# Attention into a two-layer block: order of the block sums, of the words' square, of the late parts' rests and of a load

## The chip, the cores and the metric

The kernel runs on one core of one Trainium2 chip. The core has a matrix engine (TensorE, PE in the profile; PEld is its weight load), VectorE (DVE), ScalarE (ACT), GpSimd (POOL), and SyncE (SP), which here only issues DMAs. Each engine works through its own instructions in order and waits on semaphores for the others. The metric is the device time of one execution in microseconds: the median of several.

## The reference

Eight sequences of 448 positions and 12 heads of 64 go through attention; the result, 3584 x 768, goes through two large products with a squared ReLU between them.

```python
q_n, k_n = rmsnorm(q, g_q), rmsnorm(k, g_k)        # x / sqrt(mean(x*x) + 1e-6) * g
scores = (q_n @ k_n.T) / sqrt(64)
attn = exp(scores - max(scores));  attn = attn / (sum(attn) + 1e-9)
x = (attn @ v) laid out as 3584 x 768
h = x @ w_in                                       # 768 x 2048, w_in arrives as float64
g = s * maximum(h, 0) ** 2 + b
out = g @ w_out                                    # 2048 x 768, w_out arrives as float64
```

## The kernel before, in words

**Three stages.** Stage A (0 to about 600 us of the profiled span) is attention, two heads (a *pair*) at a time, 48 pairs, in *slots*: four slots to a pair, 192 slots and some at either end. Stage B (about 605 to 1127 us) is x @ w_in, stage C (to the end) g @ w_out.

**Stage A.** A table, `STAGES` (L30), and the calls of `at` (L379 to L392) say in which slot each step of a pair is issued; within a slot, steps stand in the order in which they were put down. Steps that matter here, for pair p, with s0 = 4p: `load_kq` (L210, DMA of k, q and v of the pair, 704 KB, into one of six buffers `kqv`; the buffer is free when `weigh`, L286, of pair p-6 has read it); `scale` (L223: ScalarE multiplies k by a constant, L226, then GpSimd multiplies k and q by the rows' norms, L230); `score` and `maximum` (L237, L249: products into the one PSUM tile `sh`, then VectorE takes maxima, L253); `score_t` and `exponent`; `weigh`; `take` (L308: ScalarE copies the weighted sums to `uz` and the sums of exponentials to `sz`, L316, one buffer); `gather` (L319, DMA `s_d` from `sz`) two slots later, `fetch` (L322, DMA `zt` from `s_d`) two slots after that, `invert` (L326, VectorE, L328 and L329) three slots after that, then `put_z`, `get_z`, `divide` (GpSimd, L344) and `put_x`. Most DMAs are issued by SP, in order; `raw` (L189) by ScalarE's queue. Every DMA carries one of eight semaphores (DMAHW0 to DMAHW7) in turn, and is issued only when the DMA that carried the same one before it has landed.

**Float64 weights.** `words_of` (L107) makes float32 out of the two 32-bit words of a float64: three VectorE operations shift and join them (L110, L112, L114), ScalarE squares the high word (L116), and a fourth VectorE operation (L119) zeroes what is too small, by that square. Of w_in this happens in stage A (`convert`, L349; its square is one row apart from the other steps, a slot each). Of w_out, 32 pieces are done in stage B (`convert_out`, L567): a piece's load is started in one block and all its operations follow in the next. Each two pieces share a tile `o` (one buffer, pool "c"); after the second, GpSimd makes three sums (L138 to L140) and a DMA stores them to `w_d`.

**Stage B.** 56 *blocks*, n = 0 to 55, four to a *run* (14 runs). `ffn_in` (L468) gives TensorE 63 products for a block, into four PSUM banks of two parts each; there are eight banks, so block n+1 can begin when the sums of block n-1 have read theirs. `rectify` (L508) of block n-1 is issued after the products of block n: `add_up` (L482) makes four block sums out of seven parts (parts 0 and 1 lie in the first bank, 2 and 3 in the second): three ScalarE copies (L487 to L489), VectorE sums (L485), a fourth ScalarE copy with a changed sign (L495), more VectorE sums, eight in all; then ScalarE's ReLU (L524) and a DMA to `r_d`. Where two engines read one PSUM bank, the second waits until the first has done with it. Behind `rectify` in each engine's order stand the words of w_out (in the first three blocks of a run), and `steps` (L705): in the second block of a run GpSimd's sums for two of the next run's three inputs and the first `s_split` (L454: ScalarE rounds, L150, VectorE takes the rest, L152), in the third block GpSimd's sums of the third input, in the last block two more `s_split`. In blocks 25 to 28 `steps` also makes four late parts of w_in ready: 12 `tin_split` (L541), ScalarE rounding and VectorE taking the rest. Each part goes into the buffer of a part that TensorE has just read for the last time, and is read three blocks after the block in which it is made. The pieces of w_out are begun from block 4 on, but not in a run's third block; the last is finished in block 46.

**Stage C.** 112 rounds of 21 products, `multiply` (L632); after each eighth, `combine` (L651) makes the block sums by the same `add_up`, here with one PSUM bank a part, and stores them.

The order on every engine is the order of the calls in the program (`manual_schedule`, L676): nothing is moved by a scheduler.

## Time and profile before

| | |
|---|---|
| time, median of 3 runs | 1562.89 us (1559.93 to 1564.72) |
| profiled execution, its own time | 1566.36 us |
| its span | 1564.6 us |
| PE / PEld busy | 1385.4 us (89%) / 1101.2 us (70%) |
| DVE / ACT / POOL busy | 1000.1 / 773.4 / 807.5 us |
| DMA | 253.71 MB, mean 162 GB/s |
| granted PE clock, mean | 0.952 |

The span is the time between the first and the last instruction of the profiled execution; 1.8 us lie around it. A group's line gives busy time and mean time of one instruction, then, behind the bar, how long the engine stood idle just before such instructions and what ended that. In a timeline row the idle time before the first instruction of the row stands in brackets. The granted clock is 1.00 at 2.4 GHz and 0.50 at 1.2 GHz.

### The profile page before, as it was taken

What the parts mean: (1) busy time and instruction counts of PE and PEld (TensorE: products, weight loads), DVE (VectorE), ACT (ScalarE), POOL (GpSimd) and SP (SyncE); (2) the same over time, 40 slices, a digit from 0 to 9 for tenths busy, and PEclk for the clock granted to TensorE, in tenths of its full rate; (3) what the DMA queues carried; (4) which work ended last, traced back from release to release, by engine and by line L of the source; (5) the groups of instructions that cost most, each with busy time, mean ns of one, the idle gap of its engine ahead of it and who ended that gap; (6) DMA issues with size and microseconds to landing.
All of it is one profiled execution on the core that took longest, in us unless ns stands there. A gap on an engine that the chain in (4) does not pass through costs nothing.

```text
span 1564.6 us, 26152 instructions
## 1 busy us (share of the span) xinstructions
PE 1385.4 (89%) x9760; PEld 1101.2 (70%) x9760; DVE 1000.1 (64%) x1546; ACT 773.4 (49%) x1132; POOL 807.5 (52%) x719
## 2 busy tenths in 40 slices
PE   2699898899898998989887789889889999999999
PEld 1344444444343446888887789879879999999999
DVE  3467575666555633566666867676687767767776
ACT  2367666666564653344444533444554444444443
POOL 5457677777666634443433433433035654654653
PEclk6799999999999999999999998999989999999999
DMA  6468786878787833444547444554653332332331
GB/s 204 127 180 227 199 237 193 232 204 246 216 230 209 231 103 105 152 166 147 169 145 263 151 160 143 166 172 140 215 187 95 116 100 82 117 99 83 115 99 63
DMA packets 172367, 253.71 MB, mean 162 GB/s; under 512 B 54544, under 2 KB 122832, under 8 KB 172240
## 3 DMA queue, kind: packets, MB, share of 16 engines
q1 hardware_dynamic: 165904, 231.86, 48.8%
q10 hardware_dynamic: 6336, 20.19, 4.4%
q8 instruction: 76, 1.25, 0.3%
q14 instruction: 51, 0.42, 0.1%
HBM read 183.06 MB, written 68.76 MB: 161 GB/s over the span
## 4 chain that ended last, share of the span: by engine, by line
PE 47%; DMA 16%; DVE 12%; issue 11%; ACT 6%; POOL 5%; SPq 2%; ACTq 0%; POOLq 0%; DVEq 0%
PE m L642 24%; PE st L273 6%; PE av L294 6%; PE h L476 4%; DMA zt<-s_d 3%; DVE r L485 3%; DMA raw<-in_dram 3%; PE sh L244 3%; PE av L301 2%; ACT s L150 2%; DVE nmx L253 2%; DVE s L152 2%; PE st L277 2%; DMA s<-x_d 2%; DMA i_d<-ri 2%
## 5 line engine op out<-in xcount | busy, mean ns | idle before, releaser
L476 PE MATMUL h<-s,tin 128*128 128x256 f32 x3528 | 457.9, 293 | 68.6 <-DVE r L485 39.2
L476 PEld LDWEIGHTS h<-s,tin 128*128 128x128 f32 x3528 | 446.3, 198 | 80.8 <-DVE r L485 46.3
L642 PE MATMUL m<-tout,gh 128*128 128x384 f32 x1568 | 405.6, 340 | 8.2 <-ACT gh L626 7.9
L642 PEld LDWEIGHTS m<-tout,gh 128*128 128x128 f32 x1568 | 288.0, 190 | 9.7 <-ACT gh L626 8.7
L253 DVE TENSOR_REDUCE nmx<-sh 112x2 fp32r<-112x896 f32 x192 | 207.8, 1084 | 109.9 <-PE sh L244 106.9
L642 PE MATMUL m<-tout,gl 128*128 128x384 f32 x784 | 266.7, 340 | 5.7 <-DVE gl L627 5.7
L284 ACT ACTIVATE e<-st 128x896 f32<-128x896 f32 x192 | 176.3, 919 | 146.9 <-PE st L277 146.6
L606 POOL TENSOR_TENSOR g<-g 128x256 f32<-128x256 f32 x112 | 94.4, 843 | 230.7 <-DVE g L605 230.7
L626 ACT CAST gh<-g 128x896 fp32r<-128x896 f32 x112 | 105.4, 942 | 175.1 <-POOL g L610 101.3
L273 PE MATMUL st<-kqv 64*128 64x448 f32 x768 | 188.2, 563 | 0.0
L627 DVE TENSOR_TENSOR gl<-g,gh 128x896 fp32r<-128x896 f32 x112 | 140.8, 1258 | 58.6 <-ACT gh L626 58.6
L244 PEld LDWEIGHTS sh<-kr 64*112 64x112 f32 x384 | 55.8, 278 | 168.2 <-issue 58.1
L294 PE MATMUL av<-e,kqv 128*32 128x448 f32 x1536 | 165.1, 547 | 7.5 <-ACT uz L317 5.2
L485 DVE TENSOR_TENSOR r<-r,h 128x256 f32<-128x256 f32 x408 | 144.0, 415 | 37.0 <-ACT r L495 26.3
L244 PE MATMUL sh<-kr 64*112 64x448 f32 x384 | 94.2, 481 | 80.1 <-DVE nmx L253 41.7
L152 DVE TENSOR_TENSOR s<-s,s 128x1792 fp32r<-128x1792 f32 x42 | 84.5, 2037 | 122.6 <-ACT s L150 114.1
L642 PEld LDWEIGHTS m<-tout,gl 128*128 128x128 f32 x784 | 149.0, 190 | 7.8 <-DVE gl L627 7.8
L277 PE MATMUL st<-shq,row 64*128 64x448 f32 x384 | 145.7, 742 | 3.8 <-DMA shq<-nmx 3.8
L344 POOL TENSOR_TENSOR uz<-uz 128x448 f32<-128x448 f32 x48 | 65.1, 1357 | 149.3 <-DMA uz<-z_d 149.3
L203 POOL TENSOR_TENSOR ri<-ri,mhalf 128x14 f32<-128x14 f32 x48 | 137.2, 2859 | 4.0
L138 POOL TENSOR_TENSOR o<-o 128x384 f32<-128x384 f32 x16 | 16.2, 1011 | 238.1 <-DVE o L119 184.3
L610 POOL TENSOR_TENSOR g<-g 128x256 f32<-128x256 f32 x112 | 133.5, 1192 | 0.0
(78 smaller groups left out, 1676.2 us busy)
## 6 DMA issues: line engine op xcount, KB each, us to landing
kqv<-in_dram SPq DMA_DIRECT2D x48, 704.0 KB
raw<-r_d SPq DMA_DIRECT2D x112, 256.0 KB
r_d<-r SPq DMA_DIRECT2D x51, 512.0 KB
rb<-i_d SPq DMA_DIRECT2D x96, 224.0 KB
raw<-in_dram ACTq DMA_DIRECT2D x44, 448.0 KB
w64i<-in_dram SPq DMA_DIRECT2D x24, 512.0 KB
w64o<-in_dram SPq DMA_DIRECT2D x32, 384.0 KB
uz<-z_d SPq DMA_DIRECT2D x96, 112.0 KB
```

The costliest lines, as they stand in the source:

```text
L203: G.tensor_tensor(ri, ri, mhalf[:, :n], ALU.pow)
L244: T.matmul(sh[:QC, j, :SEQ], t[d, 1].rearrange("k (p c) -> k c p", c=NQ)[:, c], t[d, 0], start=True, stop=True,)
L253: V.tensor_reduce(out=nmxs[p][:, :, c : c + 1], in_=shs.pop(i)[:QC, :, :SEQ], op=ALU.max, axis=AX.X, negate=True,)
L273: T.matmul(st[:, j, :SEQ], t[d, 0, k0 : k0 + P], t[d, 1], start=True, stop=False)
L277: T.matmul(st[:, j, :SEQ], row[d], shq[p % 3][d], start=False, stop=True)
L284: S.activation(e, sts.pop(i)[:, :, :SEQ], AF.Exp)
L294: T.matmul(t[n * Q : (n + 1) * Q, 0, :SEQ], x[:, 2 * g + h, j, m * Q : (m + 1) * Q], e[h][:, j], start=g + h == 0, stop=g + h == 2,)
L476: T.matmul(to, w[:, lw, sa], x[:, lx, tb], start=k == n == 0 and j % 2 == 0, stop=k == NK - 1 and n == 2, skip_group_check=True,)
L485: V.tensor_tensor(to, to, part(j), op_)
L610: G.tensor_tensor(g9[:, 5:7], g9[:, 0:9:8], g9[:, 1:8:6], ALU.subtract)
L627: V.tensor_tensor(gl, g9[:, 1:8], gh.bitcast(F32), ALU.subtract)
L642: T.matmul(to, g[:, sa], w, start=m == 0 and n == 0, stop=m == NM - 1 and n == 2,)
```

## The change

- `add_up`: the four ScalarE copies stand in a run (part 0, part 1, part 0 again, part 3), then the eight VectorE sums; the sums themselves are the same.
- `words_of`: ScalarE's square comes first and writes into a part of the output tile that is not yet in use, instead of over the low words after VectorE's third operation.
- `tin_split`: the 12 rests are taken on GpSimd instead of VectorE.
- The pieces of w_out are begun from block 2 on (block 3, as third blocks are left out), but none in blocks 24 to 28; the last is finished in block 50. A piece's operations can no longer be drawn forward by the slots of attention that lie in blocks 0 to 6.
- `load_kq` is issued three slots later (-8 instead of -11), and at the start not before slot -12.
- `sz` has two buffers, one of them in another pool, taken in turn.

```diff
--- before.py
+++ after.py
@@ -31,7 +31,7 @@
     "raw": (-21, 0),
     "norm": (-16, 1),
     "keep": (-13, 3),
-    "kq": (-11, 1),
+    "kq": (-8, 2),
     "spread": (-10, 4),
     "scale": (-5, 5),
 }
@@ -104,16 +104,15 @@
     w_d = [[dpool.tile([P, 7 * HC], F32, name=f"w_d{m}_{h}") for h in range(2)] for m in range(NM)]
     i_d = [dpool.tile([2, 2 * SEQ], F32, name=f"i_d{p}") for p in range(NPAIR)]
 
-    def words_of(a, w):
+    def words_of(a, w, m):
 
         low, high = w
+        S.activation(m, high.bitcast(F32), AF.Square)
         V.tensor_scalar(a, high, 3, 0x3FFFFFF8, ALU.logical_shift_left, ALU.bitwise_and)
         yield
         V.scalar_tensor_tensor(a, high, -0x40000000, a, ALU.bitwise_and, ALU.bitwise_or)
         yield
         V.scalar_tensor_tensor(a, low, 29, a, ALU.logical_shift_right, ALU.bitwise_or)
-        m = low.bitcast(F32)
-        S.activation(m, high.bitcast(F32), AF.Square)
         yield
         af = a.bitcast(F32)
         V.scalar_tensor_tensor(af, m, LEAST * LEAST, af, ALU.is_ge, ALU.mult)
@@ -146,10 +145,10 @@
             tin[q] = wpool.tile([P, NK, 2, 7, P], F32R, tag=f"s{q % QUADS}", name=f"tin{q}")
         return tin[q]
 
-    def split(to, of):
+    def split(to, of, E=V):
         S.copy(to[0], of)
         yield
-        V.tensor_tensor(to[1], of, to[0].bitcast(F32), ALU.subtract)
+        E.tensor_tensor(to[1], of, to[0].bitcast(F32), ALU.subtract)
 
     def begin():
         S.activation(warm, mhalf[:, 0:1], AF.Exp)
@@ -312,7 +311,7 @@
             else:
                 uz = lp.tile([P, 2 * TG], F32, tag="uz", bufs=4, name=f"uz{p}")
             uzs[p] = uz
-            sz = szs[p] = lp.tile([P, SEQ], F32, tag="sz", name=f"sz{p}")
+            sz = szs[p] = (lp if p % 2 else ap).tile([P, SEQ], F32, tag="sz", name=f"sz{p}")
             S.copy(sz, t[:, 1, :SEQ])
             S.copy(uz[:, :SEQ], t[:, 0, :SEQ])
 
@@ -356,7 +355,10 @@
             for _ in range(6):
                 yield
             t = ep.tile([P, 9, P], F32, tag="t9", bufs=2, name=f"t9_{n}")
-            yield from words_of(four(t, P).bitcast(I32), (w[:, :, :, 0], w[:, :, :, 1]))
+            yield from words_of(
+                four(t, P).bitcast(I32), (w[:, :, :, 0], w[:, :, :, 1]),
+                t[:, 2:6].rearrange("p (h c) f -> p h (c f)", h=2),
+            )
             sums_left(t, G)
             yield
             yield
@@ -479,31 +481,27 @@
                         skip_group_check=True,
                     )
 
-    def add_up(c11, c12, c21, c22, part, done=None):
-
-        def add(to, j, op_):
-            V.tensor_tensor(to, to, part(j), op_)
-
-        S.copy(c11, part(0))
+    def add_up(c11, c12, c21, c22, part, done=lambda j, h: None):
+
+        def add(to, a, j, op_):
+            V.tensor_tensor(to, a, part(j), op_)
+
         S.copy(c22, part(0))
         S.copy(c21, part(1))
-        add(c22, 1, ALU.subtract)
-        add(c21, 2, ALU.add)
-        if done:
-            done(0, 1)
-        add(c11, 2, ALU.add)
+        S.copy(c11, part(0))
         S.activation(c12, part(3), AF.Copy, scale=-1.0)
-        add(c22, 3, ALU.subtract)
-        add(c12, 4, ALU.add)
-        if done:
-            done(1, 0)
-        add(c11, 4, ALU.subtract)
-        add(c22, 5, ALU.add)
-        if done:
-            done(0, 0)
-        add(c11, 6, ALU.add)
-        if done:
-            done(1, 1)
+        add(c22, c22, 1, ALU.subtract)
+        add(c21, c21, 2, ALU.add)
+        done(0, 1)
+        add(c11, c11, 2, ALU.add)
+        add(c22, c22, 3, ALU.subtract)
+        add(c12, c12, 4, ALU.add)
+        done(1, 0)
+        add(c11, c11, 4, ALU.subtract)
+        add(c22, c22, 5, ALU.add)
+        done(0, 0)
+        add(c11, c11, 6, ALU.add)
+        done(1, 1)
 
     def rectify(r, g, q):
 
@@ -541,7 +539,7 @@
     def tin_split(n):
         q, k = divmod(n, NK)
         to = t_in(QUADS + q)
-        return split((to[:, k, 0], to[:, k, 1]), staged[0][:, n % 6])
+        return split((to[:, k, 0], to[:, k, 1]), staged[0][:, n % 6], G)
 
     touts = {}
 
@@ -577,7 +575,10 @@
         if nh == 0:
             o9s[k] = pools["c"].tile([P, 9, HC], F32, tag="o9", name=f"o9_{k}")
         t = o9s[k]
-        yield from words_of(t[:, nh : nh + 8 : 7].bitcast(I32), (w[:, :, :, 0], w[:, :, :, 1]))
+        yield from words_of(
+            t[:, nh : nh + 8 : 7].bitcast(I32), (w[:, :, :, 0], w[:, :, :, 1]),
+            t[:, 2 + 2 * nh : 4 + 2 * nh],
+        )
         if nh:
             sums_right(t, G)
             yield
@@ -749,11 +750,12 @@
                     s_load(NK * (r + 1) + 1)
                 elif i == 2:
                     s_load(NK * (r + 1) + 2)
-            begun_, begun[:] = begun[:], []
-            if n >= 4 and todo and i != 2:
+            begun_, fresh = begun[:], []
+            begun.clear()
+            if n >= 2 and todo and i != 2 and not 24 <= n < 29:
                 c = convert_out(todo.pop(0))
                 next(c)
-                begun.append(c)
+                fresh.append(c)
             if n:
                 rectify(*blocks[n - 1])
             for u in range(3 * n, 3 * n + 3):
@@ -761,6 +763,7 @@
                     slot(NSLOT + 2 + u)
             for x in begun_:
                 finish(x)
+            begun.extend(fresh)
             steps(n)
             if n == nb - QUADS - 1:
                 assert not todo and not begun
```

**ScalarE in stage B, the block sums of the third block of run 5.** `r` is the tile of sums, `h` the PSUM parts, `w64o` the raw words of w_out, `o` their output tile; L524 (L522 in the changed kernel) is the ReLU, L487 to L489 and L495 (L489 to L492) are the four copies, L116 (L110) is the square. Before:

```order
L524 ACTIVATE r_1_7895<-r_1_7895 128x1024 [waits DVE_49]
L116 ACTIVATE w64o_7793<-w64o_7793 128x384 [waits DMAHW6_49,DVE_49,Activation_49]
L487 COPY r_2_7994<-h_2_0_7825 128x256 [waits PE_49]
L488 COPY r_2_7994<-h_2_0_7825 128x256
L489 COPY r_2_7994<-h_2_0_7825 128x256
L495 ACTIVATE r_2_7994<-h_2_1_7826 128x256 [waits DVE_49,PE_49]
L524 ACTIVATE r_2_7994<-r_2_7994 128x1024 [waits DVE_49]
```

And now:

```order
L522 ACTIVATE r_1_7906<-r_1_7906 128x1024 [waits DVE_49]
L110 ACTIVATE o_7_7921<-w64o_7801 128x384 [waits DMAHW7_49,DMAHW1_49,Activation_49]
L489 COPY r_2_8002<-h_2_0_7836 128x256 [waits DMAHW0_49,PE_49]
L490 COPY r_2_8002<-h_2_0_7836 128x256
L491 COPY r_2_8002<-h_2_0_7836 128x256
L492 ACTIVATE r_2_8002<-h_2_1_7837 128x256 [waits PE_49]
L522 ACTIVATE r_2_8002<-r_2_8002 128x1024 [waits DVE_49]
```

The fourth copy waited for VectorE and for TensorE, and now waits for TensorE alone; the square waited for VectorE's third operation, and now for DMAs and an earlier square.

**SP in stage A, around the store of pair 20's sums.** `shq` takes the maxima, `s_d` stores `sz`, `kqv` is the load of k, q and v, `zt` the fetch of the sums, `z_d`, `uz`, `x_d` the later steps, `rb` the rows' norms. The semaphore that a DMA waits for first is its own of the eight. Before:

```order
L262 DMA shq_345<-nmx_2779 1x112x4 [waits DMAHW0_49,DVE_49]
L262 DMA shq_345<-nmx_2779 1x112x4 [waits DMAHW1_49]
L320 DMA s_d_159<-sz_2886 4x448 [waits DMAHW2_49,Activation_49]
L212 DMA kqv_2925<-in_dram 128x1408 [waits DMAHW4_49,PE_49]
L347 DMA x_d_133<-uz_2546 128x448 [waits DMAHW5_49,Pool_49]
L338 DMA uz_2658<-z_d_205 64x448 [waits DMAHW6_49]
L338 DMA uz_2658<-z_d_205 64x448 [waits DMAHW7_49]
L219 DMA rb_2961<-i_d_302 64x896 [waits DMAHW0_49]
L219 DMA rb_2961<-i_d_302 64x896 [waits DMAHW1_49]
L333 DMA z_d_206<-zt_2863 128x7 [waits DMAHW2_49,DVE_49]
L324 DMA zt_2976<-s_d_159 128x2x7 [waits DMAHW3_49]
```

And now:

```order
L261 DMA shq_345<-nmx_2777 1x112x4 [waits DMAHW7_49,DVE_49]
L261 DMA shq_345<-nmx_2777 1x112x4 [waits DMAHW0_49,PE_49]
L211 DMA kqv_2904<-in_dram 128x1408 [waits DMAHW1_49,PE_49]
L319 DMA s_d_159<-sz_2885 4x448 [waits DMAHW2_49,Activation_49]
L346 DMA x_d_133<-uz_2544 128x448 [waits DMAHW3_49,Pool_49]
L337 DMA uz_2657<-z_d_205 64x448 [waits DMAHW4_49]
L337 DMA uz_2657<-z_d_205 64x448 [waits DMAHW5_49]
L218 DMA rb_2959<-i_d_302 64x896 [waits DMAHW6_49]
L218 DMA rb_2959<-i_d_302 64x896 [waits DMAHW7_49]
L332 DMA z_d_206<-zt_2862 128x7 [waits DMAHW0_49,DVE_49]
L323 DMA zt_2974<-s_d_159 128x2x7 [waits DMAHW2_49,DMAHW1_49]
```

The load of k, q and v stood behind the store of the sums, and now stands before it, and three slots later. DMAHW3, missing between `s_d` and the load before, is that of `raw`, which ScalarE's queue issues there: the fetch `zt` waited for it. Now `zt` waits for the semaphore of the load of k, q and v (DMAHW1), besides that of the store it reads; where a load of w_in's words lies between, it is `z_d` that waits for the load of k, q and v.

**The rests of w_in's late parts, blocks 25 and 26.** On VectorE before (`s` is the rest of an input of the next run, `tin` of a late part of w_in, `r` the block sums):

```order
L119 SCALAR_TENSOR_TENSOR o_7_8107<-w64o_8090,o_7_8107 128x2x192 [waits Activation_49]
L152 TENSOR_TENSOR s_8214<-s_21_8084,s_8214 128x1792 [waits DMAHW3_49,DMAHW2_49,Activation_49]
L152 TENSOR_TENSOR tin_8217<-staged,tin_8217 128x896 [waits DMAHW4_49,Activation_49]
L152 TENSOR_TENSOR tin_8217<-staged,tin_8217 128x896 [waits DMAHW5_49,Activation_49]
L152 TENSOR_TENSOR tin_8217<-staged,tin_8217 128x896 [waits DMAHW0_49,Activation_49]
L485 TENSOR_TENSOR r_1_8297<-r_1_8297,h_1_0_8115 128x256 [waits Activation_49]
L485 TENSOR_TENSOR r_1_8297<-r_1_8297,h_1_1_8116 128x256 [waits PE_49]
L485 TENSOR_TENSOR r_1_8297<-r_1_8297,h_1_1_8116 128x256
L485 TENSOR_TENSOR r_1_8297<-r_1_8297,h_1_1_8116 128x256 [waits Activation_49]
```

On GpSimd now (`s` rows are the three sums of an input):

```order
L137 TENSOR_TENSOR s_22_8095<-s_22_8095 128x512 [waits DMAHW6_49,DMAHW5_49,Pool_49]
L138 TENSOR_TENSOR s_22_8095<-s_22_8095 128x256
L139 TENSOR_TENSOR s_22_8095<-s_22_8095 128x512
L151 TENSOR_TENSOR tin_8215<-staged,tin_8215 128x896 [waits Activation_49] x2
L151 TENSOR_TENSOR tin_8215<-staged,tin_8215 128x896 [waits DMAHW1_49,Activation_49]
L137 TENSOR_TENSOR s_23_8292<-s_23_8292 128x512 [waits DMAHW7_49,DMAHW0_49,DVE_49]
L138 TENSOR_TENSOR s_23_8292<-s_23_8292 128x256
L139 TENSOR_TENSOR s_23_8292<-s_23_8292 128x512
L151 TENSOR_TENSOR tin_8313<-staged,tin_8313 128x896 [waits DMAHW2_49,Activation_49]
L151 TENSOR_TENSOR tin_8313<-staged,tin_8313 128x896 [waits DMAHW1_49,Activation_49]
L151 TENSOR_TENSOR tin_8313<-staged,tin_8313 128x896 [waits DMAHW2_49,Activation_49]
```

Three `tin` rows stood between `s` and the block sums on VectorE; now they stand on GpSimd behind the sums of the next run's inputs.

## Rows read from the trace of the kernel before

**Rows 1.** Busy time by stretch: share of 100 us, PE clock, DMA share, GB/s.

```profile
300.00:400.00 100.00, 90.13 (x707) 41.86 (x701) 62.24 (x84) 61.44 (x84) 75.50 (x60) 0.98 0.80 225
700.00:800.00 100.00, 89.86 (x675) 87.71 (x676) 67.32 (x132) 42.42 (x72) 36.42 (x34) 0.91 0.48 158
```

**Rows 2.** Groups by line, PE: busy, mean ns of one | idle before, releasers.

```profile
L476 PE MATMUL h<-s,tin 128*128 128x256 f32 x3528 | 457.9, 293 | 68.6 <-DVE r L485 39.2 <-DVE s L152 17.5 <-ACT s L150 6.9
```

**Rows 3.** Groups by line, block sums, words and rests, on VectorE and ScalarE.

```profile
L485 DVE TENSOR_TENSOR r<-r,h 128x256 f32<-128x256 f32 x408 | 144.0, 415 | 37.0 <-ACT r L495 26.3 <-ACT r L489 10.7
...
L487 ACT COPY r<-h 128x256 f32<-128x256 f32 x51 | 18.3, 359 | 0.0
...
L495 ACT ACTIVATE r<-h 128x256 f32<-128x256 f32 x51 | 19.6, 385 | 106.6 <-DVE r L485 106.6
...
L119 DVE SCALAR_TENSOR_TENSOR o<-w64o,o 128x384 f32<-128x384 f32 x32 | 21.3, 665 | 20.3 <-ACT w64o L116 20.3
...
L152 DVE TENSOR_TENSOR tin<-staged,tin 128x896 fp32r<-128x896 f32 x12 | 17.0, 1468 | 0.5 <-ACT tin L150 0.5
```

**Rows 4.** VectorE in order of time, 936 to 1015 us: start, us, what [idle before <- releaser].

```profile
936.62 2.04 DVE L152 TENSOR_TENSOR s<-s,s 128x1792 fp32r<-128x1792 f32 x1 [7.58 <-ACT s L150]
...
940.17 1.75 DVE L485 TENSOR_TENSOR r<-r,h 128x256 f32<-128x256 f32 x5 [0.51 <-ACT r L495]
...
942.81 1.52 DVE L114 SCALAR_TENSOR_TENSOR o<-w64o,o 128x384 int32<-128x384 int32 x1
...
968.94 0.77 DVE L110 TENSOR_SCALAR o<-w64o 128x384 int32<-128x384 int32 x1 [2.92 <-DMA w_d<-o]
...
980.71 0.56 DVE L114 SCALAR_TENSOR_TENSOR o<-w64o,o 128x384 int32<-128x384 int32 x1
...
981.95 0.56 DVE L119 SCALAR_TENSOR_TENSOR o<-w64o,o 128x384 f32<-128x384 f32 x1 [0.68 <-ACT w64o L116]
...
1012.58 2.06 DVE L152 TENSOR_TENSOR s<-s,s 128x1792 fp32r<-128x1792 f32 x1 [7.60 <-ACT s L150]
```

**Rows 5.** TensorE in order of time, 640 to 1130 us.

```profile
675.81 19.96 PE L476 MATMUL h<-s,tin 128*128 128x256 f32 x166 [1.29 <-DVE s L152]
...
826.07 19.96 PE L476 MATMUL h<-s,tin 128*128 128x256 f32 x166 [1.11 <-DVE s L152]
...
914.66 19.96 PE L476 MATMUL h<-s,tin 128*128 128x256 f32 x166 [1.07 <-DVE s L152]
...
1069.80 57.34 PE L476 MATMUL h<-s,tin 128*128 128x256 f32 x481 [1.56 <-DVE s L152]
```

**Rows 6.** Groups by line, GpSimd.

```profile
L230 POOL TENSOR_TENSOR kqv<-kqv,rb 128x448 f32<-128x448 f32 x95 | 126.5, 1351 | 12.9 <-ACT kqv L226 12.3 <-DMA i_d<-ri 0.6
...
L140 POOL TENSOR_TENSOR s<-s 128x512 f32<-128x512 f32 x42 | 67.3, 1602 | 0.0
```

**Rows 7.** Who waited for whom, 0 to 605 us, TensorE: us, times, longest.

```profile
PE sh L244 <- DVE nmx L253: 41.7, 29, 4.2
```

**Rows 8.** Who waited for whom, 0 to 605 us, ScalarE.

```profile
ACT sz L316 <- DMA s_d<-sz: 44.7, 19, 4.9
```

**Rows 9.** Who waited for whom, 0 to 605 us, VectorE.

```profile
DVE zt L328 <- DMA zt<-s_d: 77.3, 30, 5.8
```

**Rows 10.** Who waited for whom, 0 to 605 us, SyncE's DMA queue.

```profile
SPq L212 <- PE av L294: 61.0, 24, 11.4
SPq L324 <- DMA raw<-in_dram: 31.8, 9, 5.8
```

**Rows 11.** Chain that ended last, in order of time: start, us, what.

```profile
233.24 3.25 DMA zt<-s_d
...
343.34 5.26 DMA kqv<-in_dram
...
390.68 7.40 DMA zt<-s_d
...
1183.27 377.81 PE m L642 x2161
```

**Rows 12.** Groups by line, ScalarE, scaling of k.

```profile
L226 ACT ACTIVATE kqv<-kqv,gqk 128x448 f32<-128x448 f32 x48 | 31.9, 665 | 1.3 <-DMA kqv<-in_dram 1.3
```

## The prediction

> **What bounds the kernel now.** I read the stretches first, then the groups by line, the orders of VectorE and TensorE in time, the waits of stage A, the chain. In both stretches of [rows 1] TensorE is at 90%, yet it has gaps, and after them its clock falls to 1.2 GHz for a while: granted 0.91 in 700 to 800 us. In stage C nothing is lost: from 1183 us to the end the chain is 2161 products in 377.8 us [rows 11], all TensorE. So a gain must come from stages A and B.
>
> *Stage B is VectorE's.* TensorE's products there have 68.6 us of idle time before them, 39.2 until VectorE's block sums and 24.4 until the split of an input [rows 2]. The first ScalarE copy of a block sum has no idle time in 51 blocks [rows 3]: when ScalarE gets to a block, TensorE has long finished it. Nobody in the loop waits for TensorE; it waits for the loop of VectorE, ScalarE and GpSimd. That loop repeats every two runs: VectorE starts the rest of a run's first input at 936.62 and again, two runs on, at 1012.58 us [rows 4], so eight blocks take 75.96 us. TensorE needs less: where it isn't held, 481 products take 57.34 us [rows 5], 0.119 us each, and eight blocks of 63 are 60.1 us. The difference of 16 us in two runs is open to the change, and VectorE's waits in these 76 us are where it must be found.
>
> *Stage A is held by small transfers.* TensorE waits 41.7 us for VectorE's maxima, in 29 stalls [rows 7]. VectorE stands 77.3 us at the fetched sums `zt`, in front of those maxima [rows 9]; ScalarE stands 44.7 us for the one `sz` buffer to be stored [rows 8]; SP stands 61.0 us at the load of k, q and v, whose buffer is not yet free, and 31.8 us at the fetch, behind `raw`, whose semaphore it shares [rows 10]. Everything that SP issues behind these comes late.
>
> **The change part by part.**
>
> *Four copies in a run.* The fourth copy waited for VectorE's third sum and VectorE's fourth for that copy: 0.51 us a block (940.17 in [rows 4]); in all 26.3 us of idle time, which over 51 blocks is 0.52 [rows 3]. Now the fourth copy runs beside VectorE's first sum. That first sum still waits for the third copy, as they read one bank, so nothing more is gained. ScalarE's 106.6 us before the fourth copy [rows 3] go too, but what follows there, the ReLU, waits for VectorE's last sum as before. Eight blocks: 4.1 us. One of the eight is lost again: a piece's first operation stood 2.92 us for the store of the shared tile (968.94 in [rows 4]), and that store ends no sooner. 3.6 us remain.
>
> *The square first.* VectorE stood 0.68 us before the fourth operation of a piece (981.95 in [rows 4]; 20.3 us over 32 pieces in [rows 3]). The square now follows the ReLU at once, whose end I put 0.1 us behind VectorE's third operation (it takes 1.06 us from the last sum, and VectorE's three operations take about 1.5), so about 0.55 us go. Five such pieces in two runs give 2.8. For the sixth, behind the store, the square also stood in ScalarE's order before the rounding of the next input, for which VectorE then waited 1.0 us more; I count 1.7. Sum 4.5 us.
>
> So 76.0 - 3.6 - 4.5 = 67.9 us for eight blocks, above TensorE's 60.1: VectorE remains the bound there, and each microsecond taken off it counts in full, 4.0 us a run. Unchanged is the longest wait, 7.60 us before 1012.58 [rows 4]: VectorE stands for a rounding that stands for GpSimd, whose sums of a piece and of an input lie one behind the other. Fully loaded both before and after are eight runs (the third to sixth and the ninth to twelfth counted from one): 675.81 to 826.07 and 914.66 to 1069.80 [rows 5], 305.4 us. Gain: 8 x 4.0 = 32 us.
>
> *Late parts on GpSimd, no pieces in blocks 24 to 28.* The two runs between, 826.07 to 914.66, took 88.6 us [rows 5]. VectorE loses 12 rests of 1.47 us [rows 3] and most of the pieces there, so TensorE is the bound, at 60 us. GpSimd gets 12 rests of 896 columns; at 1351 ns for 448 [rows 6] each takes 2.7 us, 32 in all, beside three inputs' sums of 1280 columns, 3.9 each: 44 us in blocks 25 to 28, which last 30. Nobody reads a late part for three blocks, which hides this, but GpSimd ends about 14 us late, and in block 29 the next sums stand behind it; VectorE's rest of that input waits, and the block sums behind that. I price that at 6 us (between 0, if the rests take 2.2 us each, and 14). Gain 88.6 - 66 = 22 us.
>
> The [rows 4] show one operation of a piece at 1.52 us (942.81) where it takes 0.56 alone (980.71). The Trainium skill (SBUF — State Buffer, section Who interferes with whom) says that a VectorE instruction with two SBUF inputs and a GpSimd instruction that reads SBUF exclude each other for a whole instruction. The rows agree. By this rule three rests of inputs in these blocks could each stand for one late rest, 8 us more, and the time would come to 1493 instead of the 1485 below.
>
> *Pieces later.* The thirteenth run gets three pieces that it did not have, and the second run a third one: 4 and 1.5 us lost.
>
> Stage B in sum: 32 + 22 - 5.5 = 48 us. Bounds: 25, if contention with GpSimd eats half of the loaded runs' gain and of the late parts'; 65, if the loop also shortens where it waits for GpSimd.
>
> *The load three slots later, and two `sz` buffers.* A pair takes 80 products (counts of the page), and 707 in 100 us [rows 1] make 11.3 us a pair, 2.8 a slot. The buffer is now free when SP arrives, so the 61.0 us at SP go, and with two buffers ScalarE's 44.7. The 31.8 us behind `raw` turn into waits behind the load of k, q and v, which is issued three slots before the fetch, while `raw` went out only shortly before it. What was hidden and may come out: `scale` now follows the load by three slots instead of six, some 8 us. The load took 5.3 us where the chain shows it [rows 11], and ScalarE's scaling waited 1.3 us for it in all [rows 12]. So mostly covered; a load that takes 10 us stops ScalarE, and everything behind it, for 2. Bounds of the gain: nothing at all, and the 41.7 us of [rows 7] with some 10 us of slow clock (granted 0.98 in [rows 1]), 52. The waits named by the rows are just those that the edits remove, but transfers stay slow under this load: `zt`, 7 KB, took 3.25 us in one place and 7.40 in another [rows 11]. I take 30.
>
> The DMA engines are busy 80% in stage A, at 225 GB/s [rows 1]. The Trainium skill (DMA: Bandwidth & Descriptors, section Issuing engines are not separate DMA queues) says that all issuing engines' transfers run interleaved on the same 16. By that a load moved along SP's order relieves nobody, and stage A gains as much as the freed issues allow and no more; taken strictly, nothing, which is the first rival.
>
> *The rest.* The copies' new order in stage C is hidden under TensorE [rows 11]; the words of w_in lose a ScalarE wait in stage A that nobody on the path shared. Both at 0.
>
> **Sum.** 48 + 30 = 78 us off the profiled execution's 1566.4 (span 1564.6 and 1.8 around it) gives 1488. The median of the runs shown lies 3.5 us below the profiled one; so 1485.
>
> **The rivals.**
> 1. *Stage A gains nothing*: its transfers are held by the DMA engines, not by SP's order. For it the 80% and the 7.40 us for 7 KB; against it the 61.0 and 44.7 us, which are waits for a buffer, not for a transfer. Time 1562.9 - 48 = 1515. 20%.
> 2. *Stage B gains half*, as GpSimd and VectorE hold each other up more when they are closer, or GpSimd's 44 us become the bound of two runs. For it the 1.52 us; against it that the loaded runs' GpSimd work is unchanged. 1562.9 - 25 - 30 = 1508. 13%.
> 3. *Both gain almost all*: 65 + 48, 1450. For it, that half of stage B's waits hang on VectorE alone; against it the 7.60 us. 12%.
> 4. *Slower: the load comes too late for `scale`.* Each of 42 pairs then stops ScalarE, with scores, exponentials and copies behind it in one order. Two score tiles and the two slots between exponential and use give about 3 us of cover, so it costs (landing - 8 - 3) a pair. To eat up stage B's 48 us it takes 1.1 us a pair: a usual landing of over 12.1 us, twice the 5.3 of [rows 11]. At 13 us the time is 1562.9 - 48 + 84 = 1599. 4%.
>
> **How the numbers follow.** My forecast has 51%, the rivals 20, 13, 12 and 4. The range 1452 to 1522 holds the forecast's own (1465 to 1505) and the first two rivals and reaches close to the third. A measurement of this kernel can tell 0.3%, 4.7 us, from no change. Only the fourth rival is slower, but it need not go so far: 4% slower, 3% for a landing near the point where it evens out, 93% faster.
>
> **What would show it.** Right: the block sums' idle time until the fourth copy gone, eight sums without a gap; VectorE's period of two runs in stage B near 68 us; blocks 24 to 31 without VectorE at `tin`; SP's wait at the load under 15 us and ScalarE's for `sz` near 0; TensorE's wait for maxima about halved. Wrong: a period still above 73 us; long idle time at L225, `scale`, until the load; TensorE waiting for GpSimd's rests; stage A still ending at about 600 us.

## The result, and the profile after

The changed kernel takes 1466.9 us (median; 1465.4 to 1470.7), the kernel before, run beside it, 1561.4 (1559.6 to 1564.7): ratio 0.940, 95% interval 0.937 to 0.942. The forecast was 1485, the range 1452 to 1522. So the direction and the range held, but two of the terms were off by a factor of nearly two, in opposite directions: that the sum came as near as 18 us is in part luck.

The span is 1463.7 us against 1564.6. To split it by stage, this is the line of x @ w_in on TensorE, in the kernel before and in the changed one; behind the durations stand the first and the last start.

```profile
L476 PE MATMUL h<-s,tin x3528: 274/281/582, 604.8 to 1126.9; 128*128 128x256 f32 x196
```

```profile
L478 PE MATMUL h<-s,tin x3528: 274/282/583, 548.1 to 1027.4; 128*128 128x256 f32 x196
```

Stage A ends 56.7 us sooner (604.8, 548.1). Stage B, from first to last product, takes 479.3 instead of 522.1, 42.8 less. What follows takes 436.3 instead of 437.7: nothing, as forecast. The granted clock rises from 0.952 to 0.972 over the span.

TensorE's busy time in stage A, as sums over 0 to 605 us before and 0 to 548 us after:

```profile
sum 605.00, PE 507.65 PEld 238.74 DVE 343.02 ACT 348.48 POOL 388.01; mean PE 72.52 PEld 34.11 DVE 49.00 ACT 49.78 POOL 55.43
```

```profile
sum 548.00, PE 496.93 PEld 231.63 DVE 342.60 ACT 348.02 POOL 394.69; mean PE 70.99 PEld 33.09 DVE 48.94 ACT 49.72 POOL 56.38
```

Some 46 us of the gain are idle time of TensorE (97.4, now 51.1), some 11 us are the same products in less busy time, at a granted clock of 0.96 instead of 0.94.

The same stretches as in [rows 1]:

```profile
300.00:400.00 100.00, 96.59 (x768) 44.37 (x764) 67.02 (x92) 67.82 (x95) 79.30 (x66) 1.00 0.91 255
700.00:800.00 100.00, 91.21 (x732) 88.98 (x732) 62.98 (x121) 50.41 (x81) 56.71 (x42) 0.98 0.57 185
```

In 300 to 400 us TensorE does 768 products where it did 707, 8.6% more, and the DMA engines, at 80% before, now carry 255 GB/s at 91%. In 700 to 800 us the granted clock is 0.98 where it was 0.91.

Groups by line, those that answer to [rows 2, 3, 12]:

```profile
L478 PE MATMUL h<-s,tin 128*128 128x256 f32 x3528 | 440.2, 287 | 40.4 <-DVE r L487 19.5 <-DVE s L151 18.4 <-ACT s L149 1.2
...
L487 DVE TENSOR_TENSOR r<-r,h 128x256 f32<-128x256 f32 x408 | 139.5, 412 | 18.1 <-ACT r L491 17.8
...
L225 ACT ACTIVATE kqv<-kqv,gqk 128x448 f32<-128x448 f32 x48 | 32.1, 668 | 17.9 <-DMA kqv<-in_dram 17.8
...
L151 POOL TENSOR_TENSOR tin<-staged,tin 128x896 fp32r<-128x896 f32 x12 | 26.8, 2265 | 0.0
...
L118 DVE SCALAR_TENSOR_TENSOR o<-o 128x384 f32<-128x384 f32 x32 | 22.8, 712 | 4.5 <-ACT o L110 0.9
...
L492 ACT ACTIVATE r<-h 128x256 f32<-128x256 f32 x51 | 20.7, 406 | 0.0
```

VectorE's sums no longer wait for the fourth copy (26.3 us before), but the wait before the first sum, at the third copy, has grown from 10.7 to 17.8; ScalarE's 106.6 before the fourth copy are gone. The fourth operation of a piece stands 4.5 instead of 20.3. GpSimd takes 2265 ns on average for a late part's rest, VectorE took 1468. ScalarE's scaling waits 17.8 us for the load (1.3 before).

GpSimd's wait for the divisors in stage A of the kernel before:

```profile
POOL uz L344 <- DMA uz<-z_d: 132.4, 43, 7.5
```

Who waited for whom in stage A of the changed kernel, those that answer to it and to [rows 7 to 9], and SP's queue, for [rows 10]:

```profile
POOL uz L343 <- DMA uz<-z_d: 31.6, 9, 8.5
...
ACT kqv L225 <- DMA kqv<-in_dram: 17.8, 12, 4.8
...
PE sh L243 <- DVE nmx L252: 9.8, 8, 2.3
...
DVE zt L327 <- DMA zt<-s_d: 1.8, 1, 1.8
```

```profile
SPq L323 <- DMA kqv<-in_dram: 7.8, 7, 2.0
...
SPq L211 <- PE sh L243: 4.5, 10, 0.9
```

TensorE's 41.7 us at the maxima are 9.8, VectorE's 77.3 at `zt` 1.8, GpSimd's wait for the divisors 31.6 (132.4 before). ScalarE no longer waits for `sz` to be stored, SP's largest wait at the load, 61.0 before, is 4.5, and the fetch, which stood 31.8 us behind `raw`, stands 7.8 behind the load.

TensorE in order of time, for [rows 5]; the first, second, fourth and fifth row are where the third, seventh, ninth and thirteenth run stall for their second input:

```profile
621.61 30.55 PE L478 MATMUL h<-s,tin 128*128 128x256 f32 x252 [1.56 <-DVE s L151]
...
754.42 31.68 PE L478 MATMUL h<-s,tin 128*128 128x256 f32 x252 [1.56 <-DVE s L151]
...
818.35 12.55 PE L478 MATMUL h<-s,tin 128*128 128x256 f32 x86 [6.50 <-DVE r L487]
831.64 30.68 PE L478 MATMUL h<-s,tin 128*128 128x256 f32 x252 [0.74 <-DVE s L151]
...
968.50 30.55 PE L478 MATMUL h<-s,tin 128*128 128x256 f32 x252 [0.75 <-DVE s L151]
```

Third to sixth run: 132.8 us (150.3 before); seventh and eighth: 77.2 (88.6); ninth to twelfth: 136.9 (155.1). VectorE's loop, for [rows 4]:

```profile
672.69 2.06 DVE L151 TENSOR_TENSOR s<-s,s 128x1792 fp32r<-128x1792 f32 x1 [7.59 <-ACT s L149]
...
739.13 2.06 DVE L151 TENSOR_TENSOR s<-s,s 128x1792 fp32r<-128x1792 f32 x1 [7.60 <-ACT s L149]
...
784.94 2.61 DVE L151 TENSOR_TENSOR s<-s,s 128x1792 fp32r<-128x1792 f32 x1 [2.71 <-ACT s L149]
791.13 2.18 DVE L151 TENSOR_TENSOR s<-s,s 128x1792 fp32r<-128x1792 f32 x1 [3.58 <-ACT s L149]
...
814.71 3.25 DVE L151 TENSOR_TENSOR s<-s,s 128x1792 fp32r<-128x1792 f32 x1 [8.90 <-ACT s L149]
```

672.69 to 739.13 is the period of eight blocks, 66.4 us (76.0 before), with the 7.60 us wait in it unchanged.

### The profile page after: what moved, and what is told of

The parts are those of the page before. It is cut to its first block, busy times and chain, and to the rows that moved or that the text cites. A ratio compares the mean times of both kernels' runs of the same rounds, so it can differ in the third digit from the quotient of the medians.

```text
span 1463.7 us, 26101 instructions
## 1 busy us (share of the span) xinstructions
PE 1357.6 (93%) x9760; PEld 1079.9 (74%) x9760; DVE 975.4 (67%) x1534; ACT 766.7 (52%) x1132; POOL 839.2 (57%) x731
## 4 chain that ended last, share of the span: by engine, by line
PE 53%; issue 12%; DMA 11%; POOL 9%; DVE 8%; ACT 4%; SPq 2%; ACTq 0%; POOLq 0%; DVEq 0%
PE m L643 26%; PE av L293 8%; PE st L272 7%; PE av L300 4%; PE sh L243 4%; DVE r L487 3%; PE h L478 3%; DMA s<-x_d 2%; POOL s L139 2%; PE st L276 2%; DVE s L151 2%; DMA to<-w_d 2%; ACT s L149 2%; POOL s L138 1%; POOL s L137 1%
## 5 line engine op out<-in xcount | busy, mean ns | idle before, releaser
L478 PE MATMUL h<-s,tin 128*128 128x256 f32 x3528 | 440.2, 287 | 40.4 <-DVE r L487 19.5
L478 PEld LDWEIGHTS h<-s,tin 128*128 128x128 f32 x3528 | 431.0, 192 | 50.5 <-DVE r L487 24.7
L628 DVE TENSOR_TENSOR gl<-g,gh 128x896 fp32r<-128x896 f32 x112 | 137.2, 1226 | 65.0 <-ACT gh L627 64.9
L272 PE MATMUL st<-kqv 64*128 64x448 f32 x768 | 179.9, 545 | 0.0
L151 DVE TENSOR_TENSOR s<-s,s 128x1792 fp32r<-128x1792 f32 x42 | 87.5, 2105 | 130.9 <-ACT s L149 122.7
L487 DVE TENSOR_TENSOR r<-r,h 128x256 f32<-128x256 f32 x408 | 139.5, 412 | 18.1 <-ACT r L491 17.8
L229 POOL TENSOR_TENSOR kqv<-kqv,rb 128x448 f32<-128x448 f32 x95 | 124.2, 1324 | 38.8 <-ACT kqv L225 13.9
L522 ACT ACTIVATE r<-r 128x1024 f32<-128x1024 f32 x51 | 54.1, 1061 | 173.9 <-DVE r L487 173.9
L202 POOL TENSOR_TENSOR ri<-ri,mhalf 128x14 f32<-128x14 f32 x48 | 141.7, 2951 | 4.0
L276 PE MATMUL st<-shq,row 64*128 64x448 f32 x384 | 139.6, 719 | 3.5 <-DMA shq<-nmx 3.5
L243 PE MATMUL sh<-kr 64*112 64x448 f32 x384 | 91.7, 474 | 35.4 <-ACT kr L234 25.3
```

What stands on the lines that cost most here:

```text
L202: G.tensor_tensor(ri, ri, mhalf[:, :n], ALU.pow)
L243: T.matmul(sh[:QC, j, :SEQ], t[d, 1].rearrange("k (p c) -> k c p", c=NQ)[:, c], t[d, 0], start=True, stop=True,)
L272: T.matmul(st[:, j, :SEQ], t[d, 0, k0 : k0 + P], t[d, 1], start=True, stop=False)
L276: T.matmul(st[:, j, :SEQ], row[d], shq[p % 3][d], start=False, stop=True)
L478: T.matmul(to, w[:, lw, sa], x[:, lx, tb], start=k == n == 0 and j % 2 == 0, stop=k == NK - 1 and n == 2, skip_group_check=True,)
L487: V.tensor_tensor(to, a, part(j), op_)
```

## The experiments

Each kernel was timed beside the kernel before (median 1565 to 1569 in these sets, 1561.4 beside the changed kernel); the ratio is to those runs, so that differences to the changed kernel come out larger by the ratios than by the times. "A" is the start of the first product of x @ w_in in the profiled execution, "B" the time from there to the last. The last three columns split B at the start of every 252nd product, 252 to a run: the eight loaded runs, the seventh with the eighth, the other four. (The 77.2 and 88.6 us above go from stall to stall, and differ by up to 1.1 us from this count.) Executions of unchanged code differ too: in the six kernels with the changed kernel's stage A, A lies between 543.8 and 551.5.

| kernel | time | ratio, 95% interval | A | B | loaded | 7+8 | others |
|---|---|---|---|---|---|---|---|
| before | | | 604.8 | 522.1 | 304.9 | 88.6 | 128.5 |
| load | 1515.9 | 0.971 (0.965 to 0.977) | 563.3 | 525.2 | | | |
| two `sz` | 1562.2 | 0.999 (0.996 to 1.001) | 593.0 | 528.1 | | | |
| load, two `sz` | 1518.7 | 0.971 (0.967 to 0.976) | 554.4 | 526.0 | | | |
| seven buffers | 1527.7 | 0.976 (0.972 to 0.980) | 565.9 | 523.7 | | | |
| square, w_in only | 1561.6 | 0.996 (0.994 to 0.998) | 598.1 | 523.7 | | | |
| square | 1528.7 | 0.979 (0.973 to 0.984) | 590.9 | 497.2 | 287.3 | 84.8 | 125.0 |
| block sums | 1532.6 | 0.978 (0.976 to 0.980) | 601.4 | 494.2 | 285.0 | 83.8 | 125.3 |
| changed kernel | 1466.9 | 0.940 (0.937 to 0.942) | 548.1 | 479.3 | 269.6 | 78.3 | 131.4 |
| rests on VectorE | 1459.6 | 0.930 (0.929 to 0.932) | 544.6 | 475.5 | 270.3 | 70.8 | 134.4 |
| the same, no gap | 1458.9 | 0.931 (0.928 to 0.933) | 543.8 | 471.8 | 265.1 | 81.3 | 125.4 |
| sums first | 1457.9 | 0.929 (0.928 to 0.931) | 549.5 | 469.3 | 256.8 | 78.5 | 134.0 |
| rests on VectorE, sums first | 1452.9 | 0.926 (0.923 to 0.929) | 551.5 | 466.0 | 261.1 | 70.8 | 134.1 |
| the same, no gap | 1447.8 | 0.924 (0.922 to 0.926) | 546.0 | 464.5 | 257.9 | 76.7 | 130.1 |

**The load alone**, on the kernel before.

```diff
-    "kq": (-11, 1),
+    "kq": (-8, 2),
```

> The kernel before with the load of k, q and v three slots later and nothing else. In the changed kernel stage A ended 56.7 us earlier (604.81 to 548.12), where I had forecast 30. Theory 'each its own wait' (mine): SP's 61.0 us at the load go, ScalarE's 44.7 us for sz stay, so stage A gains about half of the 57, 20 to 35 us, time about 1533. Rival 'SP's line': the blocked load holds all that SP issues behind it, the gather of sz among it, so that this edit alone gives 45 us or more, time 1515 or less, and ScalarE's wait for sz falls with it. Rival 'either one holds': with sz still single the pairs stay late, gain under 10 us, time over 1552. Stages B and C as before in all three.

Its waits in stage A, and SP's for a free buffer at the load:

```profile
POOL uz L344 <- DMA uz<-z_d: 34.3, 7, 8.7
...
PE sh L244 <- DVE nmx L253: 10.3, 9, 2.3
...
ACT sz L316 <- DMA s_d<-sz: 4.9, 1, 4.9
...
DVE zt L328 <- DMA zt<-s_d: 1.4, 1, 1.4
```

```profile
SPq L212 <- PE av L294: 2.4, 1, 2.4
```

One edit, and four waits are gone or small that I had put down to separate causes: SP's 61.0 us are 2.4, `zt` is at 1.4, the wait for the store of `sz` at 4.9, though there is still one `sz` buffer, and the divisors fall from 132.4 to 34.3. The gain is 45 us by the ratio. (The profiled execution was the slowest of its four, 1527.5 where the others took 1514.6 to 1516.5, so its A of 563.3 is some 12 us late.) This is "SP's line", at the lower edge of what I gave it. ScalarE's place is less clear than the row of `sz` says. Its idle time before that copy, whatever ended it, in the kernel before and with the later load:

```profile
L316 ACT COPY sz<-av 128x448 f32<-128x448 f32 x48 | 25.4, 529 | 58.3 <-DMA s_d<-sz 44.7 <-PE av L301 8.8 <-PE sh L244 4.2
```

```profile
L316 ACT COPY sz<-av 128x448 f32<-128x448 f32 x48 | 25.6, 532 | 49.1 <-PE av L301 9.2 <-PE st L277 8.2 <-DMA uz<-z_d 5.5
```

Most of it stays and is now put down to others, while the time falls by 45 us; with two buffers alone (below) it falls to 18.3 us, and the time does not. So this idle time was not what held stage A.

**Two `sz` buffers alone.**

```diff
-sz = szs[p] = lp.tile(...)
+sz = szs[p] = (lp if p % 2 else ap).tile(...)
```

> The kernel before with two sz buffers and nothing else. 'Each its own wait': ScalarE's 44.7 us go, SP's 61.0 stay: 15 to 30 us off stage A, time about 1540. 'SP's line': ScalarE waited for a gather that SP issued late; without that wait the transfers stay as late as they were, under 8 us, time over 1554. 'Either one holds': under 10 us as well, but then the load alone gives under 10 too.

```profile
DVE zt L328 <- DMA zt<-s_d: 76.1, 33, 5.9
```

```profile
SPq L212 <- PE av L294: 52.0, 25, 12.0
```

ScalarE no longer waits for the store, and little else changes: VectorE stands 76.1 us at `zt` (77.3 before), SP 52.0 at the load (61.0). The interval holds no change. What little could be there is below the measurement: the profiled A is 11.8 us earlier, but B is 6.0 longer, and ten timed runs show no gain.

**Both.** (The two diffs together.)

> The kernel before with both, the later load and two sz buffers, without the rest of the change. If these two make all of stage A's gain: 52 to 60 us, time 1503 to 1511, stage A ending near 548. 'Each its own wait' wants this to be the sum of the two edits alone within 6 us; 'SP's line' wants it within 8 us of the load alone; 'either one holds' wants it over 25 us above the sum of the two. If the square of w_in's words has a part in it, it is under 48 us here.

0.971 as with the load alone: the second `sz` buffer is worth nothing that can be measured, before or after the load is moved. It is also 45 us and not the 57 of the profile, so that stage A seems to owe a part to something else.

**Seven buffers for the load, issued as early as before.**

```diff
-tag="kq", bufs=6
+tag="kq", bufs=7
```

> The kernel before with seven buffers for k, q and v instead of six, the load issued as early as before. The later load alone gave 47 us. Theory 'SP's line': what cost was that SP stood at a load whose buffer was not yet free, and the gathers and fetches behind it; a seventh buffer frees it four slots sooner, so the 61.0 us at the load, the 77.3 at zt and the 39.8 at sz go here as well and the time is 1510 to 1525. Rival 'place': the early load itself is in the way, as its 704 KB run ahead of the small transfers on the DMA engines; then it is over 1545.

```profile
ACT sz L316 <- DMA s_d<-sz: 4.8, 1, 4.8
...
DVE zt L328 <- DMA zt<-s_d: 1.9, 1, 1.9
```

With the early load but a free buffer the waits for `zt` and for the store of `sz` go as well, SP no longer waits at the load for TensorE's `av`, which frees the buffer, and the gain is 38 us; the interval overlaps that of the later load. So it is, for the most part at least, not the place of the load in time that cost, but SP standing in front of a buffer that isn't free, with gathers, fetches and shifts behind it in its order. The time lies 3 us above what I expected; whether the early load's own traffic costs those few us isn't told by this run.

**The square first**, in both kinds of words, and in the words of w_in (stage A) alone.

```diff
+        S.activation(m, high.bitcast(F32), AF.Square)
         V.tensor_scalar(a, high, ...)
...
-        m = low.bitcast(F32)
-        S.activation(m, high.bitcast(F32), AF.Square)
```

> The kernel before with the square ahead of the three shifts and nothing else. For stage B my term is 4.5 us in eight loaded blocks, 18 us over the eight loaded runs, and about 3 more in the others: time about 1543. For stage A my forecast was nothing; a rival for the 27 us that I missed there is that ScalarE's wait for the words' third operation, in line with exponentials and copies, held the loop: then stage A ends 10 us or more before 604.8, and the time is 1530 or less.

> The kernel before with the square ahead of the three shifts in the words of w_in alone, which are made in stage A; the words of w_out as before. With the square ahead in both, the time fell by some 36 us, of which 25 in stage B, where I had forecast 21. Theory 'the wait at the square held stage A': ScalarE stood 16.1 us in 11 stalls before the square, with exponentials and copies behind it; without them stage A ends 8 to 16 us sooner, time 1549 to 1557, stage B unchanged. Rival, my own forecast that nobody on the path shared that wait: within 4 us of before, and stage A's earlier end in the last run was its scatter.

The square in both kinds of words takes 1528.7 us, where I expected 1543; all of stage B is 24.9 us shorter (21 forecast), and the eight loaded runs lose 17.6 us, where I had 18. VectorE's period, by the same wait in two runs:

```profile
680.21 2.05 DVE L151 TENSOR_TENSOR s<-s,s 128x1792 fp32r<-128x1792 f32 x1 [7.60 <-ACT s L149]
...
751.04 2.05 DVE L151 TENSOR_TENSOR s<-s,s 128x1792 fp32r<-128x1792 f32 x1 [7.59 <-ACT s L149]
```

70.8 us, 5.1 less than before (forecast 4.5). In stage A I had counted nothing, and there it ended at 590.9. By time and stage A's end the rival holds; the second run asks how much of that is scatter. The wait was in the trace of before, in a row that I passed over:

```profile
ACT w64i L116 <- DVE t L114: 16.1, 11, 3.8
```

With the square first in w_in's words alone the time falls by 6 us (0.996; interval 3 to 9), with stage B unchanged at 523.7. That is clear of nothing, but the interval reaches into both readings, within 4 us and 8 to 16. Nor is this wait apart from SP's line. With the load alone, the square as before, it is already small:

```profile
ACT w64i L116 <- DVE t L114: 4.4, 10, 1.0
```

So how much of these 6 us is left once the load is moved, no run here shows.

**The block sums alone.**

```diff
-        S.copy(c11, part(0))
         S.copy(c22, part(0))
         S.copy(c21, part(1))
+        S.copy(c11, part(0))
+        S.activation(c12, part(3), AF.Copy, scale=-1.0)
...
-        S.activation(c12, part(3), AF.Copy, scale=-1.0)
```

> The kernel before with the four copies of the block sums in a run and nothing else. My term: 4.1 us in eight blocks less 0.5 that the store of the shared tile takes back, 14 us over the eight loaded runs, and a few more in the other runs: 14 to 20 us, time about 1547; VectorE's 26.3 us before its fourth sum gone. Rival, that the two waits at the store and at the rounding take most of it back, as they stand behind GpSimd: under 7 us, time over 1558. Rival, that ScalarE's fourth copy was also what held the ReLU and the words behind it: over 24 us.

```profile
915.82 2.06 DVE L152 TENSOR_TENSOR s<-s,s 128x1792 fp32r<-128x1792 f32 x1 [7.60 <-ACT s L150]
...
985.94 2.05 DVE L152 TENSOR_TENSOR s<-s,s 128x1792 fp32r<-128x1792 f32 x1 [7.59 <-ACT s L150]
```

The time falls by 34 us by the ratio, where I expected 14 to 20. The period is 70.1 us, 5.8 less, where my term was 3.6; the loaded runs lose 19.9 us (14 forecast), all of stage B 27.9; what is left can't be told from scatter. Summing VectorE's rows over the two periods: its waits fall by 3.5 us, which is the term, and its own operations by 2.3, 0.95 of it in the third shift of a piece, 0.7 in the fourth, 0.75 in the sums. The same operations took less time; why is not shown. (The 0.95 are one third shift of 1.52 us, as at 942.81 in [rows 4], that is now 0.56.) The number is that of the third reading, over 24 us, but its mechanism is not there: VectorE's waits before the fourth operation of a piece, for the square behind the ReLU, are 4.06 us in the period before and 4.07 now.

**The late parts' rests on VectorE again**, in the changed kernel.

```diff
-    return split((to[:, k, 0], to[:, k, 1]), staged[0][:, n % 6], G)
+    return split((to[:, k, 0], to[:, k, 1]), staged[0][:, n % 6])
```

> The changed kernel with the rests of the 12 late parts on VectorE again; pieces of w_out as in the changed kernel, none in blocks 24 to 28. In the changed kernel the seventh and eighth runs took 77.2 us together, where I had 66, and the eighth 44.0. Theory 'GpSimd is late' (mine, with the price too small): the rests, 2.27 us each there, put GpSimd's next sums off, and the wait of 6.5 us at 818 us stands for it; on VectorE, which has no pieces there, 12 rests of 1.47 us find room, the eighth run falls to 33 to 37 us and the time to 1456 to 1461. Rival 'VectorE is late': the block sums stand behind the rests and TensorE behind the block sums: time 1467 or more.

What it mends is seen in GpSimd's order of time in the changed kernel:

```profile
785.63 2.51 POOL L138 TENSOR_TENSOR s<-s 128x256 f32<-128x256 f32 x1
...
789.34 20.47 POOL L151 TENSOR_TENSOR tin<-staged,tin 128x896 fp32r<-128x896 f32 x9
...
811.01 0.73 POOL L138 TENSOR_TENSOR s<-s 128x256 f32<-128x256 f32 x1
...
814.82 1.26 POOL L139 TENSOR_TENSOR s<-s 128x512 f32<-128x512 f32 x1
```

Nine rests keep GpSimd for 20.47 us; only then do its sums for the next inputs come. VectorE waits 8.90 us for that input (814.71 above), its block sums come behind, and TensorE stands 6.50 us (818.35). With the rests on VectorE the eighth run has no such stall:

```profile
L151 DVE TENSOR_TENSOR tin<-staged,tin 128x896 fp32r<-128x896 f32 x12 | 16.1, 1395 | 3.9 <-ACT tin L149 3.9
```

```profile
788.74 33.09 PE L478 MATMUL h<-s,tin 128*128 128x256 f32 x252 [1.38 <-DVE s L151]
823.38 30.55 PE L478 MATMUL h<-s,tin 128*128 128x256 f32 x252 [1.56 <-DVE s L151]
```

The rests take 16.1 us there, and VectorE has room. 7.3 us faster than the changed kernel by the times, 14 by the ratios, and the intervals do not meet; the seventh and eighth runs of the profile are 7.5 shorter. Moving the rests to GpSimd was a loss of some 7 us at the least.

**No gap for the pieces**, with the rests on VectorE: the block sums, the square, the load and `sz` alone (and the pieces' operations no longer drawn forward).

```diff
-            if n >= 2 and todo and i != 2 and not 24 <= n < 29:
+            if n >= 4 and todo and i != 2:
```

> The changed kernel with the rests of the late parts on VectorE and the pieces of w_out in every block from the fourth on, as before; that is the block sums, the square, the load and sz alone. With the rests on VectorE but no pieces in blocks 24 to 28 it took 1459.6, and its seventh and eighth runs 71.0 us. Theory 'the sums and the square account for most of stage B': each alone brought these two runs from 88.7 to about 84.7, so both make 81, and the pieces' gap gives 10 of the 22 us that I had put to it; 3 to 5 us of that go back in the runs that get the pieces: time 1463 to 1467. Rival, my own sum (22 us from the gap and the rests): 84 us or more in the two runs, 1472 or more. Rival, the gap gives nothing: 1459 or less.

```profile
769.85 12.58 PE L478 MATMUL h<-s,tin 128*128 128x256 f32 x84 [8.14 <-DVE r L487]
```

1458.9 against 1459.6. The seventh and eighth runs take 81.3 instead of 70.8, with this stall of 8.14 us, and the others give 14.2 back (5.2 in the loaded ones, 9.0 in the rest). The 81 was expected, the size of what goes back was not, and so the last of the three readings holds: the gap moves work and gains nothing that can be measured here.

**GpSimd's sums of two inputs first**, ahead of a piece's sums, in the changed kernel.

```diff
+            if r + 1 < len(runs) and i == 1:
+                s_sums(NK * (r + 1))
+                s_sums(NK * (r + 1) + 1)
             for x in begun_:
                 finish(x)
...
-                    s_sums(s0)
-                    s_sums(s0 + 1)
```

> The changed kernel with GpSimd's sums for two inputs, in the second block of a run, ahead of its sums of a piece of w_out in that block instead of behind them. Theory: VectorE's 7.6 us before an input's rest, which it spends in every second run waiting for ScalarE's rounding and so for GpSimd, is GpSimd's order alone. Without it the period of two runs, 66.3 us, falls to 60 to 62, where TensorE is the bound; four such pairs make 16 to 24 us, and two more stalls outside them a few: time 1440 to 1450. Rival: the store of the shared tile goes out later by GpSimd's 8 us, and the next piece's first operation stands for that store instead (3.49 us there now): within 5 us of 1467, or slower.

```profile
601.67 2.02 DVE L151 TENSOR_TENSOR s<-s,s 128x1792 fp32r<-128x1792 f32 x1 [1.02 <-ACT s L149]
...
667.19 2.02 DVE L151 TENSOR_TENSOR s<-s,s 128x1792 fp32r<-128x1792 f32 x1 [1.03 <-ACT s L149]
...
702.52 2.02 DVE L151 TENSOR_TENSOR s<-s,s 128x1792 fp32r<-128x1792 f32 x1
```

At the rest of a run's first input VectorE stands at most 1.03 us in the loaded runs, where it stood 7.60 in every second one: that wait was GpSimd's order. (The ninth is apart: its 8.94 us stand behind the late parts' rests, as the 8.90 at 814.71 above.) The loaded runs lose 12.8 us, less than the 16 I wanted at the least, and the time of 1457.9 lies between the two readings. The rival has a share in it: with the sums first the store of the shared tile goes out later, and VectorE's waits at the next piece's first operation grow from 3.5 to 6.3 us between 601 and 667 us.

**Both of the last edits, and both without the gap.** (The diffs above together.)

> The changed kernel with both later edits: the rests of the late parts on VectorE, and GpSimd's sums of two inputs ahead of a piece's in the second block of a run. If they act in different runs, as their traces say (the eighth run for the one, the loaded runs for the other), they add: 1467 less 7 and 9, 1448 to 1453. If both only free GpSimd of the same lateness, 1456 to 1460.

> As the kernel with the rests on VectorE and GpSimd's sums of two inputs first (1452.9), but with pieces of w_out in every block from the fourth on. Without that order of GpSimd's sums the gap gave nothing: 1458.9 without it, 1459.6 with it, as the 10 us that it saved in the seventh and eighth runs were lost in the others, which got the pieces. Theory 'the gap only moves work': the same here, 1450 to 1456, with some 9 us more in the seventh and eighth runs (70.4 there now) and as much less in the others. Rival 'the loaded runs are TensorE's now': with the sums first they have no more to give back when the pieces leave them, so that the gap is worth its 9 us and this kernel takes 1459 or more. Rival: VectorE's order around the late parts gains from the new order too, under 1449.

They add: 1452.9. Without the gap it is 1447.8, lowest of all and below what I expected, though the interval overlaps that with the gap. It is not VectorE's order around the late parts that gained, as the third reading wanted: the seventh and eighth runs take 6 us more, and the others 7 less. The profiled executions differ by 8.5 us, but 5.5 of them lie in stage A, where the code is the same, and only 1.5 in stage B. So it is not shown that leaving out the gap gains anything here.

The lowest time is that of the block sums, the square and the load of this change, with GpSimd's sums first and without the late parts' rests on GpSimd and the gap (it keeps the second `sz` buffer): 0.924.

## Why the prediction was right, and where it was not

- *Stage A, 30 forecast, bounds 0 and 52; 56.7 in the profile.* The mis-sized term. The step that failed was the bound and the choice below it: I bounded the gain by TensorE's own wait for maxima, and took 30 because "transfers stay slow under this load". They do stay slow: in the chain of the changed kernel, start, us, what:

```profile
282.43 5.09 DMA zt<-s_d
...
348.72 7.21 DMA kqv<-in_dram
```

  A 7 KB fetch still takes 5 us, and the load 7.2, more than the 5.3 of [rows 11]. But VectorE hardly stands at the fetch any longer (1.8 us); ScalarE's 17.8 at the load cost less than the rest gained. The 77.3 us at `zt` and the 61.0 at the load had one cause, SP's line (load alone, 45 us), and the 44.7 at `sz` were not a cost of their own. TensorE's wait for maxima fell by 31.9 us (41.7 to 9.8) and its busy time by some 11, about the 10 that I had for the slow clock; the other 14 us are idle time at other places, which the bound of 52 left out. The words' square alone gave 6; as its wait shrinks with the load alone, 45 and 6 can't simply be added, and what makes up the rest of the 56.7, beside the differences of A between executions, stays open. My "both at 0" was wrong for the square, and so was the part that I gave to `sz`.
- *The loaded runs, 32 forecast; 35.3 by the count.* Right, and in the main by the right steps: the period was to be 67.9 and is 66.4. VectorE's waits in it fall by 7.7 us, where the two terms have 8.1; the other 1.8 are its own operations, which took less time and of which the forecast knew nothing. Taken alone, the square's term held (4.5; 5.1), the block sums' was too small (3.6; 5.8).
- *The seventh and eighth runs, 22 forecast; 11.4.* The second mis-sized term. The larger error is its floor: "TensorE is the bound, at 60 us" holds in no kernel here. Even with the rests back on VectorE the two runs take 70.8 (33.6 and 37.2); there the 252 products from 788.74 us on take 33.09 us, where the next 252 take 30.55. The price of GpSimd's lateness, 6 us, was nearly right (7.5 in these two runs), but not its lower end: it was to be nothing with rests of 2.2 us each, and they took 2.27. (By the prediction's own figures, 12 of 2.2 and 11.7 of sums make 38 us in blocks that last 30, so that end should have been 8.) Of the signs of error that I had named, TensorE waiting for GpSimd's rests, the 6.50 us at 818.35 are one, by way of VectorE. Some 7 us of the gain come from the block sums and the square there (81.3 with these alone); the gap's own 10 are given back elsewhere.
- *Later pieces, 5.5 forecast.* The four runs outside took 2.9 us more in the changed kernel, but they also have the gain of the sums and the square: with the rests on VectorE they take 9.0 more with the gap than without it. The price was too low.
- *The rivals.* "Stage A gains nothing" fell: the DMA share rose with the rate. The Trainium skill (DMA: Bandwidth & Descriptors, section Issuing engines are not separate DMA queues) says that the transfers of all issuing engines interleave on the same 16. That a moved load then relieves no transfer is my reading, and the trace agrees with it: the transfers above are no faster than before. But taken strictly, as nothing to gain, the reading was wrong: seven buffers, which free the issues and leave the load as early as it was, gain 38 us. "Slower, the load too late for `scale`" has its mechanism in the row of L225, 17.8 us in stage A, but the waits were at most 4.8 us and TensorE's own for ScalarE's `kr` did not grow (30.1 us before, 25.3 now). The third rival, both almost all, was right for stage A only (56.7 for its 48; stage B 42.8 for its 65).
- *The rule on SBUF* (the Trainium skill, SBUF — State Buffer, section Who interferes with whom) was to cost VectorE 8 us at three rests. These took 2.61, 2.18 (791.13) and 3.25 us where 2.02 is usual: 2 us in all. Only the one at 791.13 stood beside late parts, the others beside GpSimd's sums of inputs. The trace shows the exclusion more on GpSimd: the sum at 785.63 took 2.51 us beside VectorE's rest at 784.94, and 0.73 at 811.01 alone; the late rest that began at 791.39, beside the one at 791.13, took 3.89, the other eleven 2.09 to 2.14.
